# Token sums of the last stage taken from the transposes' PSUM, waits that order GpSimd, and conversions all in the second stage

## Chip, cores and metric

One core of a Trainium2 chip. Times are device microseconds of that core; a run is the time of one whole execution. The kernel before has a median of 644.73 us over 3 runs (643.39 to 645.41).

## What is computed

Three stages follow one another on 1152 tokens of 512 features:

```python
x = window_attention(q, k, v)                 # 2 x 8 heads, 576 positions, window of 64
p = probs / probs.sum(-1)                     # 4 experts
y = sum(p[:, e] * (relu(x @ w1[e]) @ w2[e]) for e in range(4))   # 512 -> 1024 -> 512
h = y @ w_in                                  # 512 -> 2048
out = (h * cos(h)) @ w_out                    # 2048 -> 512
```

The inputs are float32, but `w_in` and `w_out` come as 64-bit floats and are turned into 32-bit ones on the chip.

## The kernel before

**Arithmetic.** Every matmul is done three times: each operand is split into a high part (rounded to the fast 32-bit type) and a low part (the remainder), and high x high, high x low and low x high are added in PSUM. ScalarE writes the high parts and VectorE or GpSimd the low ones.

**Stages.** Attention is a script written out by hand. After it the work is cut into chunks `c` of 512 hidden features: chunks 0 to 7 (NM = 8) are the mixture of experts (two per expert), chunks 8 to 11 the last stage. Tokens are cut into two sets `k`: set 0 has 640 tokens (n = SN[0] = 320 columns in each half, 5 tiles of 128) and set 1 has 512 (n = 256, 4 tiles). A visit (c, k) has two units `u`, and a unit is a first product (`a_unit`) and a second (`b_unit`). The sets alternate: (7,1), (7,0), (8,1), (8,0) are the visits around the turn from the experts to the last stage.

**First product.** `a_unit` multiplies 2 x 2 blocks with seven block products instead of eight (p1 to p7, of 6 matmuls each, at L1049). Product 1 reads the first half of the tokens (`xhi`, `xlo`, features 0 to 255), 2 the same tokens with features 256 to 511, 3 the second half with features 256 to 511, and 5, 6, 7 and 4 read sums of token blocks: `tsum` is formed from `xhi` and `xlo`, and its high and low parts go to `xhi`/`xlo` (second half, features 0 to 255) and `thi`/`tlo`. `t_jobs` makes these sums: for each group of up to 128 columns eight additions or subtractions in a chain (L963, L972), two casts on ScalarE (L985), two remainders (L988). They run on VectorE or GpSimd.

**After the first product** come ReLU in the experts (L1141) and in the last stage `h * cos(h)` (`cos_post`: L1157, L1162, L1168, L1169, L1174, L1177, L1183, three of them on VectorE). `b_unit` then multiplies by the second weights into accumulators (L1236, 6 matmuls per token tile and unit), and `evict` adds these to `acc` on VectorE.

**The turn.** After chunk 7, `turn` transposes each token tile of `acc` into PSUM (`psx`, L1304); ScalarE writes `xhi` (L1312) and VectorE `xlo` (L1317), scaled by 1/2π. Then `t_jobs` makes the sums from `xhi` + `xlo` and all products of (8, k) wait for all of them. For both sets these sums wait for `cos_ready` too, the point from which the last stage's buffers exist; it comes after the conversions.

**Conversions.** Each 64-bit weight unit is loaded, put together from its words on VectorE (L737, L743, L753, L759, L770, with one step on ScalarE, L750, and one sum on GpSimd or VectorE, L765), and stored to DRAM as 32 bits (L776). Twelve of the 16 units run in the experts' stage as 24 parts of 512 columns; the last four (`late_conversions`) run in the last stage as 16 parts of 256. Loads and stores go over SyncE's queue, with the weights.

**Order.** A planner in the kernel's Python makes jobs with an engine, an estimated duration and predecessors, plays them through on a model of the engines and emits each engine's instructions in the order in which the jobs began there. TensorE's list is fixed up to a look-ahead of 8. A job made by `either` may go to VectorE or GpSimd. Jobs marked `port` (GpSimd's, and VectorE's with operands in SBUF alone) never overlap in the plan, but nothing on the chip holds GpSimd to that: it starts as soon as its own inputs are there. GpSimd takes no job in the plan while more than QUIET port jobs of VectorE are ready. `Slots` counts buffers (raws 4, banks 3, accs 4, tsums 2) and `Hold` keeps one of them until its last user is done.

Of the kernel before, what the change touches and what calls it, by code (L numbers as in the profile page):

```python
# [26 lines left out]
def tile_window_attention_moe_cosglu(  # L27
# [13 lines left out]
    P = 128  # L41
# [22 lines left out]
    GC = [G0[g] - S0[SG[g]] for g in range(NG)]  # L64

# [263 lines left out]
    def att_xhi(u):  # L329
        pv, at = o_t[u], (u - 1) * W  # L330
        k = max(i for i in range(2) if S0[i] <= at)
        if at == S0[k]:
            x_tiles(k)
        o = at - S0[k]
        o_t[u] = pv, xhi[k][:, :, o:o + P], xlo[k][:, :, o:o + P]
        nc.scalar.copy(out=xhi[k][:, :, o:o + P], in_=pv)
# [80 lines left out]
    def emit_a(s):  # L417
# [15 lines left out]
        hh = hp.tile([P, 640], F32R, tag="hh", name="hh")[:, :n]  # L433
        hl = hp.tile([P, 640], F32R, tag="hl", name="hl")[:, :n]
        side("h", relu_high, ps, hh)
        side("j", relu_low, s, ps, hh, hl)
# [4 lines left out]
    def relu_low(s, ps, hh, hl):  # L441
# [3 lines left out]
        h_t[s] = (hh, hl)  # L445

    def emit_b(s):
# [6 lines left out]
        for i in range(no):  # L454
            cs = slice(P * i, P * (i + 1))
# [6 lines left out]
            ops = ((hh[:, cs], whi[:, fo, :]), (hh[:, cs], wlo[:, fo, :]), (hl[:, cs], whi[:, fo, :]))  # L462
# [104 lines left out]
    def mm_ns(n):  # L567
        return 13.4 + n / 2.4
# [29 lines left out]
    tsums = Slots(2)  # L598
# [11 lines left out]
    def std_a(s):  # L610
# [18 lines left out]
        def high():  # L629
            box["hh"] = hp.tile([P, 640], F32R, tag="hh", name="hh")[:, :n]  # L630
            relu_high(box["ps"], box["hh"])

        def low():
            hl = hp.tile([P, 640], F32R, tag="hl", name="hl")[:, :n]
            relu_low(s, box["ps"], box["hh"], hl)
# [76 lines left out]
    LATE = 4 * NU // 2  # L712

    def conversion(i, part, parts, name, ready):
        e, kind, u = units[len(units) - NCV + i]
        n = KD * 256 // parts
        box = {}

        def load():
            pool = late_pools[name]  # L720
            t = pool.tile([P, n], U64, tag="raw64", name="raw64", bufs=2)
            src = unit_src(e, kind, u)
            w = src.shape[2]
            if n >= w:
                src = src[:, n // w * part:n // w * (part + 1)]
            else:
                c, f = divmod(n * part, w)
                src = src[:, c:c + 1, f:f + n]
            nc.sync.dma_start(out=t.rearrange("p (a b) -> p a b", b=min(n, w)), in_=src)
# [3 lines left out]
        def words():  # L733
            pool = late_pools[name]
            m = box["m"] = pool.tile([P, n], U32, tag="m64", name="m64", bufs=2)
            box["x"] = pool.tile([P, n], F32, tag="x64", name="x64", bufs=2)
            nc.vector.tensor_scalar(  # L737
# [4 lines left out]
        def sign():  # L742
            nc.vector.scalar_tensor_tensor(  # L743
# [8 lines left out]
        def power():  # L752
            nc.vector.tensor_scalar(  # L753
# [4 lines left out]
        def low():  # L758
            nc.vector.scalar_tensor_tensor(  # L759
# [4 lines left out]
        def total(engine):  # L764
            engine.tensor_tensor(  # L765
# [3 lines left out]
        def guard():  # L769
            nc.vector.scalar_tensor_tensor(  # L770
# [7 lines left out]
        a = job("SP", 500, load, [ready, conv_r[-2]], tail=4500.0)  # L778
# [12 lines left out]
    if wide:  # L791
        for i in range(NCV - LATE):
            for part in range(2):
                conversion(i, part, 2, "w64", swapped)

    def swap_cos():
# [5 lines left out]
            tc.tile_pool(name="tsum", bufs=2, side="right", reuse_waits="tile")  # L802
        )

    def swap_late():
        tctx.close()
        late_pools["late64"] = tctx.enter_context(
            tc.tile_pool(name="late64", bufs=1, side="right", reuse_waits="tile")
        )

    tctx = ExitStack()
    own_sums = []
# [30 lines left out]
    def w1_jobs(x, m):  # L843
# [12 lines left out]
        def sums(i):  # L856
            def fn(engine):
# [8 lines left out]
                engine.tensor_tensor(out=o, in0=a, in1=b, op=op)  # L866
# [21 lines left out]
        def low(i):  # L888
            def fn(engine):
                engine.tensor_tensor(  # L890
# [20 lines left out]
    def w2_jobs(x, m):  # L911
# [20 lines left out]
        def low(i):  # L932
            def fn(engine):
                engine.tensor_tensor(  # L934
# [13 lines left out]
    def t_jobs(k, deps_of, own=False):  # L948
        n, ready = SN[k], []

        def columns(a, w):
            c1, c2 = slice(a, a + w), slice(n + a, n + a + w)
            k1, k2 = slice(0, 2), slice(2, 4)
            hold, box = Hold(tsums if own else raws), {}

            def whole(o, ks, cs):
                def fn(engine):
                    if o == 0:
                        box["t"] = (
                            late_pools["tsum"].tile([P, 4, 2, w], F32, tag="tsum", name="tsum")  # L960
                            if own else rawp.tile([P, 4, 2, w], F32, tag="raw", name="tsum")
                        )
                    engine.tensor_tensor(  # L963
# [5 lines left out]
            def less(o, i, j):  # L969
                def fn(engine):  # L970
                    t = box["t"]
                    engine.tensor_tensor(  # L972
# [21 lines left out]
            for fn in (  # L994
                whole(0, k1, c2), whole(1, k2, c2), less(2, 1, 0), whole(3, k1, c1),
                less(0, 0, 3), less(1, 1, 0), whole(3, k2, c1), less(3, 3, 1),
# [8 lines left out]
            if own:  # L1005
                own_sums.extend(ready)
# [12 lines left out]
    def a_unit(q, c, k, u):  # L1019
# [4 lines left out]
        xr = x_ready.get((c, k), [])  # L1024
        t1, t2 = slice(0, n), slice(n, 2 * n)
# [4 lines left out]
        def rhs(i):  # L1030
# [4 lines left out]
                4: lambda: (thi[k][:, 2], tlo[k][:, 2]),  # L1035
                5: lambda: (xhi[k][:, k1, t2], xlo[k][:, k1, t2]),
                6: lambda: (thi[k][:, 0], tlo[k][:, 0]),
                7: lambda: (thi[k][:, 1], tlo[k][:, 1]),
# [20 lines left out]
        p5 = pe(ns, product(5, "y2", True), [wr[2], *xr], new=[y2])  # L1059
# [16 lines left out]
        p6 = pe(ns, product(6, "z"), [c1, wr[2]], use=zu)  # L1076
# [517 lines left out]
```

## Time and profile before

| | before |
|---|---|
| median of 3 runs | 644.73 us |
| profiled execution, its own time | 645.19 us |
| its span, first to last instruction | 643.4 us |
| VectorE busy | 482.5 us |
| ScalarE busy | 333.0 us |
| GpSimd busy | 224.3 us |
| mean granted TensorE clock | 0.991 of full speed |

The span is what the trace covers; 1.8 us of the profiled execution lie around it. Times in the trace count from the span's start. "PEclk" is the granted clock of TensorE as a share of 2.4 GHz, so 0.50 is 1.2 GHz. "PE" is TensorE's matmul row, "DVE" VectorE, "ACT" ScalarE, "POOL" GpSimd, "SP" SyncE. A figure in square brackets is the time that an engine stood idle just before an instruction, with the engine that released it.

### The profile page before, as it was taken

Reading aid. Unit: us, or ns where it says so; the run is one execution under the profiler, and the core shown is the slowest. Engines: PE = TensorE matmul, PEld = TensorE weight load, DVE = VectorE, ACT = ScalarE, POOL = GpSimd, SP = SyncE. Lnnn points to the kernel's source line nnn. Section 1 sums busy time; section 2 is a strip of 40 time slices with the busy share of each in tenths; the row PEclk is TensorE's granted clock in tenths of the full one; section 3 lists DMA queues with packets and bytes.
Section 4 is the critical chain, followed back from the end, with each engine's and each line's share of the span. In section 5 each row is a group of like instructions: output and inputs, shape, how many; then the busy total and the mean of one; then the engine's idle time right before and its main releaser. Section 6 shows DMA issues by size and latency. Waiting matters only on the chain.

```text
span 643.4 us, 10901 instructions
## 1 busy us (share of the span) xinstructions
PE 625.2 (97%) x4019; PEld 552.8 (86%) x4019; DVE 482.5 (75%) x982; ACT 333.0 (52%) x836; POOL 224.3 (35%) x232
## 2 busy tenths in 40 slices
PE   8999999999999999999999999999699999999997
PEld 7878898889898998888999899988599888989786
DVE  5858535656998888798899753698777798797764
ACT  5957312333353443343443342448598878777563
POOL 6985202211331263253433331355014245134010
PEclk9999999999999999999999999999699999999999
DMA  8943200250055426444445021011204212121112
GB/s 271 309 144 107 76 1 0 99 197 0 1 167 151 141 83 198 146 136 151 141 136 191 35 98 34 13 34 53 66 1 139 92 50 82 51 83 50 49 65 85
DMA packets 39048, 63.12 MB, mean 98 GB/s; under 512 B 3017, under 2 KB 20937, under 8 KB 38994
## 3 DMA queue, kind: packets, MB, share of 16 engines
q1 hardware_dynamic: 38178, 61.63, 30.5%
q10 hardware_dynamic: 816, 0.79, 0.4%
q8 instruction: 31, 0.51, 0.3%
q14 instruction: 23, 0.19, 0.1%
HBM read 51.66 MB, written 10.75 MB: 97 GB/s over the span
## 4 chain that ended last, share of the span: by engine, by line
PE 77%; DVE 11%; ACT 5%; issue 3%; DMA 2%; POOL 1%; POOLq 0%; SPq 0%; DVEq 0%; ACTq 0%
PE pb_acc L1236 30%; PE y L1049 17%; PE seed L1049 13%; PE pb_acc L465 7%; PE ph L624 3%; ACT e L281 1%; DVE tsum L972 1%; PE ph L428 1%; PE ph L429 1%; PE ph L430 1%; DMA raw<-in_moe_w_dram 1%; PE psv L321 1%; DVE acc L476 1%; ACT kk L1169 1%; PE pss L257 1%
## 5 line engine op out<-in xcount | busy, mean ns | idle before, releaser
L1236 PE MATMUL pb_acc<-wlo,hh 128*128 128x512 f32 x360 | 141.7, 394 | 0.3 <-POOL wlo L934 0.3
L1236 PE MATMUL pb_acc<-whi,hh 128*128 128x512 f32 x360 | 141.6, 393 | 0.0
L1236 PE MATMUL pb_acc<-whi,hl 128*128 128x512 f32 x360 | 140.3, 390 | 0.0
L1049 PE MATMUL y<-xhi,w7hi 128*128 128x256 f32 (+1 forms) x320 | 96.2, 301 | 5.2 <-DVE hl L1183 4.2
L765 POOL TENSOR_TENSOR x<-x,m 128x512 f32<-128x512 f32 (+1 forms) x35 | 41.8, 1193 | 163.4 <-DVE x L759 158.5
L1049 PE MATMUL y<-xlo,w7hi 128*128 128x256 f32 (+1 forms) x320 | 95.5, 298 | 0.4 <-DVE xlo L988 0.4
L1049 PE MATMUL y<-xhi,w7lo 128*128 128x256 f32 (+1 forms) x320 | 95.3, 298 | 0.0
L1236 PEld LDWEIGHTS pb_acc<-whi,hl 128*128 128x128 f32 x360 | 67.6, 188 | 15.3
L1049 PE MATMUL seed<-thi,w7hi 128*128 128x320 f32 (+1 forms) x240 | 72.8, 303 | 4.0 <-DVE y L1080 2.8
L1236 PEld LDWEIGHTS pb_acc<-wlo,hh 128*128 128x128 f32 x360 | 67.8, 188 | 9.8 <-POOL wlo L934 0.9
L1236 PEld LDWEIGHTS pb_acc<-whi,hh 128*128 128x128 f32 x360 | 67.7, 188 | 9.6
L1049 PE MATMUL seed<-thi,w7lo 128*128 128x320 f32 (+1 forms) x240 | 71.0, 296 | 0.0
L1049 PE MATMUL seed<-tlo,w7hi 128*128 128x320 f32 (+1 forms) x240 | 70.9, 295 | 0.0
L1049 PEld LDWEIGHTS y<-xhi,w7hi 128*128 128x128 f32 x320 | 61.1, 191 | 8.2 <-DVE hl L1183 5.2
L1049 PEld LDWEIGHTS y<-xlo,w7hi 128*128 128x128 f32 x320 | 61.2, 191 | 2.4 <-DVE xlo L988 0.7
L1049 PEld LDWEIGHTS y<-xhi,w7lo 128*128 128x128 f32 x320 | 61.0, 191 | 0.0
L476 DVE SCALAR_TENSOR_TENSOR acc<-pb_acc,gate_p,acc 128x512 f32<-128x512 f32 x63 | 46.3, 743 | 12.9 <-PE pb_acc L1236 12.1
L1049 PEld LDWEIGHTS seed<-thi,w7hi 128*128 128x128 f32 x240 | 45.3, 189 | 12.1 <-DVE y L1080 5.0
L934 POOL TENSOR_TENSOR wlo<-raw,whi 128x512 fp32r<-128x512 f32 x22 | 30.4, 1396 | 64.4 <-ACT whi L929 64.4
L1049 PEld LDWEIGHTS seed<-tlo,w7hi 128*128 128x128 f32 x240 | 45.4, 189 | 3.6
L890 POOL TENSOR_TENSOR w7lo<-sums,w7hi 128x512 fp32r<-128x512 f32 x23 | 32.4, 1410 | 43.0 <-ACT w7hi L885 26.3
L1049 PEld LDWEIGHTS seed<-thi,w7lo 128*128 128x128 f32 x240 | 45.4, 189 | 0.0
(133 smaller groups left out, 1358.9 us busy)
## 6 DMA issues: line engine op xcount, KB each, us to landing
raw<-in_moe_w_dram SPq DMA_DIRECT2D x32, 512.0 KB, 5.1
raw<-w SPq DMA_DIRECT2D x16, 512.0 KB, 3.3
raw<-in_moe_w_in_dram SPq DMA_DIRECT2D x12, 512.0 KB, 4.3
w<-x SPq DMA_DIRECT2D x24, 256.0 KB, 4.4
raw<-in_moe_w_out_dram SPq DMA_DIRECT2D x12, 512.0 KB, 4.1
vr<-in_v_dram SPq DMA_DIRECT2D x16, 256.0 KB, 4.1
out_dram<-acc SPq DMA_DIRECT2D x18, 128.0 KB, 1.7
qraw<-in_q_dram SPq DMA_DIRECT2D x16, 128.0 KB, 3.8
```

Source lines behind the costliest of these rows:

```text
L257: nc.tensor.matmul(out=out[h][W * c:W * (c + 1), p], lhsT=qts[c][rows, p, :], rhs=kts[c][rows, p, :], start=True, stop=True,)
L281: nc.scalar.activation(out=e[:, p], in_=s[:, p], func=AF.Exp, bias=nm[:, p:p + 1], scale=1.0, accum_out=sm[:, p:p + 1],)
L321: nc.tensor.matmul(out=pv[W * h:W * (h + 1), p, W * c:W * (c + 1)], lhsT=vts[c][:, P * p + W * h:P * p + W * (h + 1)], rhs=pts[h][:, p, W ...
L428: nc.tensor.matmul(out=ps, lhsT=whi[:, d, cs], rhs=xh[:, d, :], start=d == 0, stop=False)
L465: nc.tensor.matmul(out=ps, lhsT=a, rhs=b, start=first and m == 0, stop=last and m == 2)
L476: nc.vector.scalar_tensor_tensor(out=a, in0=ps, scalar=p, in1=a, op0=ALU.mult, op1=ALU.add)
L624: nc.tensor.matmul(out=ps, lhsT=a[:, d, cs], rhs=b[:, d, :], start=d == 0 and m == 0, stop=d == KD - 1 and m == 2,)
L765: engine.tensor_tensor(out=box["x"], in0=box["x"], in1=box["m"].bitcast(F32), op=ALU.add)
L890: engine.tensor_tensor(out=operand(w_lo[x], i), in0=part(i), in1=operand(w_hi[x], i).bitcast(F32), op=ALU.subtract,)
L934: engine.tensor_tensor(out=w_lo[x][:, i], in0=box["t"][:, i], in1=w_hi[x][:, i].bitcast(F32), op=ALU.subtract,)
L1049: nc.tensor.matmul(out=ps, lhsT=a[:, WI[i], d, :], rhs=b[:, d, :], start=start and d == 0 and m == 0, stop=d == 1 and m == 2, skip_group_c ...
L1236: nc.tensor.matmul(out=ps, lhsT=a[:, cs], rhs=b[:, fo, :], start=first and fo == 0 and m == 0, stop=last and fo == 1 and m == 2,)
```

## The change

- **Token sums.** `turn` now writes to `xhi` and `xlo` only what products 1, 2 and 3 read (the first half, and features 256 to 511 of the second half). A new `token_sums` forms the sums of one column group of w columns (w = 64 for set 0, 5 groups; 128 for set 1, 2 groups) as soon as the two transposed tiles that it needs are there: one ScalarE copy from PSUM, two VectorE subtractions that read PSUM, one ScalarE cast and one remainder for product 5 (`s0`), two subtractions, one cast and one remainder for products 4, 6 and 7 (`s1`). The transposes' PSUM banks (`accs`) are held until then. Set 1's sums use the weights' raw buffers and no longer wait for `cos_ready`; set 0's have 4 buffers instead of 2.
- **Products of (8, k)** wait each for what they read: 1 and 2 for `h4`, `l4`; 5 also for `s0`; 6 also for `s1`; 3 also for `h2`, `l2`.
- **Token tiles of the last expert chunk** are done in rising order.
- **Conversions.** All 16 units run as 32 parts of 512 in the experts' stage; `late_conversions` goes.
- **Order.** Each `port` instruction on GpSimd gets a wait for the last VectorE `port` instruction before it in the plan. QUIET goes from 2 to 1. The planner's price of a matmul becomes a table.
- **No other work.** The operand order in `t_jobs` and the layout of the hidden tiles are rewritten; functions return their instruction so that the wait can be added.

```diff
+    def tokens(t, k, i):
+        return t[..., P * i:P * (i + 1)]
...
     def mm_ns(n):
-        return 13.4 + n / 2.4
+        return {256: 118.3, 320: 147.0, 384: 173.5, 512: 230.5}[n]
...
-    tsums = Slots(2)
+    tsums = Slots(4)
...
-        for i in range(NCV - LATE):
+        for i in range(NCV):
             for part in range(2):
-                conversion(i, part, 2, "w64", swapped)
+                conversion(i, part)
...
-            tc.tile_pool(name="tsum", bufs=2, side="right", reuse_waits="tile")
+            tc.tile_pool(name="tsum", bufs=4, side="right", reuse_waits="tile")
...
-    def late_conversions():
-        ready = job(None, 0.0, swap_late, [cos_ready, *own_sums])
-        conv_last[:], conv_r[:] = [ready, ready], [ready, ready]
-        if wide:
-            for i in range(NCV - LATE, NCV):
-                for part in range(4):
-                    conversion(i, part, 4, "late64", ready)
...
+        if c == NM:
+            parts = [(what, j) for (kk, i, what), j in x_parts.items() if kk == k]
+            def of(*names):
+                return [j for what, j in parts if what in names]
+            xr = of("h4", "l4")
...
-        p5 = pe(ns, product(5, "y2", True), [wr[2], *xr], new=[y2])
+        p5 = pe(ns, product(5, "y2", True), [wr[2], *xr, *of("s0")], new=[y2])
...
-        p6 = pe(ns, product(6, "z"), [c1, wr[2]], use=zu)
+        p6 = pe(ns, product(6, "z"), [c1, wr[2], *of("s1")], use=zu)
...
-        p3 = pe(ns, product(3, "y2"), [u4, wr[3]], use=[y2])
+        p3 = pe(ns, product(3, "y2"), [u4, wr[3], *of("h2", "l2")], use=[y2])
...
-        for rank, i in enumerate([*range(no - 1, n // P - 1, -1), *range(n // P)]):
+        turn_here = c == NM - 1 and u == NU - 1
+        row = [*range(no - 1, full - 1, -1), *range(full)]
+        for i in sorted(row) if turn_here else row:
...
+    def token_sums(k, i, c, w, s):
+        t1, hold1, box1, of1 = s["first"]
+        t2, hold2, box2, of2 = s["second"]
+        hold, old = Hold(raws if w == P else tsums), products[NM - 1, k]
...
+        f = job("ACT", act_ns(4 * w), whole, [t1, None if w == P else cos_ready], new=[hold], use=[hold1])
+        a = job("DVE", dve_ns(2 * w), from_psum(0, k1, 1), [f, t2], use=[hold2, hold])
+        h = job("ACT", act_ns(2 * w), sum_high(0), [a, *old], use=[hold])
+        x_parts[k, c, "s0"] = either(2 * w, sum_low(0), [h], use=[hold])
+        a = job("DVE", dve_ns(2 * w), from_psum(3, k2, 0), [a, t2], use=[hold2, hold])
+        b3 = either(2 * w, less(1, 3, 1), [a], use=[hold])
+        b4 = either(2 * w, less(2, 2, 3), [a], use=[hold])
+        h = job("ACT", act_ns(6 * w), sum_high(1), [b3, b4, *old], use=[hold])
+        x_parts[k, c, "s1"] = either(6 * w, sum_low(1), [h], use=[hold])
...
-        if c == NM and (c, k) not in x_ready:
...
-            x_ready[c, k] = t_jobs(k, deps_of, True) + [
-                j for (kk, i, what), j in x_parts.items() if kk == k and what == "l"
-            ]
...
-    QUIET = 2
+    QUIET = 1
...
+    ahead = None
     for j in sorted(jobs, key=lambda j: (began[j], rank[j])):
-        if j.size:
-            j.fn(nc.vector if j.eng == "DVE" else nc.gpsimd)
-        else:
-            j.fn()
+        made = j.fn(nc.vector if j.eng == "DVE" else nc.gpsimd) if j.size else j.fn()
+        if j.port and j.eng == "POOL" and ahead:
+            tc.add_manual_dep(
+                made.ins, ahead.ins.name,
+                mybir.DependencyInfo(mybir.DependencyClass.Sync, mybir.DependencyReason.DATA),
+                reason="one engine at a time",
+            )
+        elif j.port:
+            ahead = made
```

## Rows read from the trace of the kernel before

**Rows 1.** Page part 1: busy time, share of the span and instructions of TensorE.

```profile
PE 625.2 (97%) x4019; PEld 552.8 (86%) x4019; DVE 482.5 (75%) x982; ACT 333.0 (52%) x836; POOL 224.3 (35%) x232
```

**Rows 2.** TensorE's timeline at the turn: start us, us, what [idle before <-releaser].

```profile
451.56 0.39 PE L1236 MATMUL pb_acc<-whi,hl 128*128 128x512 f32 x1
456.18 0.63 PE L1049 MATMUL y<-xhi,w7hi 128*128 128x320 f32 x1 [4.23 <-DVE hl L1183]
...
464.97 0.31 PE L1049 MATMUL y<-xhi,w7lo 128*128 128x320 f32 x1
```

**Rows 3.** Chain that ended last: start us, us, what; one product and one token tile.

```profile
470.68 1.39 PE pb_acc L1236 x6
...
477.44 0.88 PE y L1049 x6
```

**Rows 4.** Windows: length, busy time per engine (PE PEld DVE ACT POOL), PEclk, DMA.

```profile
452.00:454.00 2.00, 0.00 (x0) 0.00 (x0) 1.97 (x7) 0.86 (x3) 0.00 (x0) 1.00 0.00 0
454.00:456.00 2.00, 0.00 (x0) 0.00 (x0) 2.00 (x5) 1.03 (x3) 0.00 (x0) 0.66 0.00 0
...
464.00:466.00 2.00, 2.00 (x10) 1.87 (x10) 0.62 (x2) 0.53 (x1) 0.00 (x0) 0.78 0.20 80
```

**Rows 5.** VectorE's timeline at the turn, columns as in rows 2.

```profile
446.86 2.85 DVE L972 TENSOR_TENSOR tsum<-tsum 128x128 f32<-128x128 f32 x2
...
451.38 0.55 DVE L988 TENSOR_TENSOR tlo<-tsum,thi 128x384 fp32r<-128x384 f32 x1
...
459.58 0.42 DVE L988 TENSOR_TENSOR xlo<-tsum,xhi 128x256 fp32r<-128x256 f32 x1
```

**Rows 6.** GpSimd's timeline at the turn, columns as in rows 2.

```profile
446.83 2.60 POOL L934 TENSOR_TENSOR wlo<-raw,whi 128x512 fp32r<-128x512 f32 x2
```

**Rows 7.** Windows as in rows 4, longer stretches.

```profile
180.00:420.00 240.00, 239.48 (x1413) 215.32 (x1412) 191.19 (x346) 94.05 (x212) 84.59 (x73) 1.00 0.40 122
420.00:440.00 20.00, 19.54 (x116) 17.29 (x116) 17.87 (x32) 12.62 (x28) 8.28 (x9) 1.00 0.16 54
440.00:460.00 20.00, 13.80 (x80) 11.43 (x78) 19.85 (x45) 13.81 (x34) 7.55 (x10) 0.87 0.00 1
```

**Rows 8.** VectorE by form: busy us, mean ns, idle before.

```profile
L770 DVE SCALAR_TENSOR_TENSOR x<-raw,x 128x512 f32<-128x512 f32 x24 | 22.9, 954 | 6.9 <-POOL x L765 6.9
L743 DVE SCALAR_TENSOR_TENSOR m<-raw,m 128x512 uint32<-128x512 uint32 x24 | 18.6, 774 | 0.2
...
L759 DVE SCALAR_TENSOR_TENSOR x<-raw,x 128x512 f32<-128x512 uint32 x24 | 17.0, 707 | 0.3
...
L753 DVE TENSOR_SCALAR x<-m 128x512 uint32<-128x512 uint32 x24 | 11.0, 460 | 0.2
L737 DVE TENSOR_SCALAR m<-raw 128x512 uint32<-128x512 uint32 x24 | 10.5, 436 | 0.0
...
L1080 DVE TENSOR_TENSOR y<-seed,p 128x256 f32<-128x256 f32 x20 | 8.5, 424 | 7.5 <-PE seed L1049 3.3 <-ACT w7hi L885 2.1 <-issue 2.0
...
L988 DVE TENSOR_TENSOR xlo<-tsum,xhi 128x256 fp32r<-128x256 f32 x8 | 3.3, 414 | 0.0
```

**Rows 9.** GpSimd by form, columns as in rows 8.

```profile
L934 POOL TENSOR_TENSOR wlo<-raw,whi 128x512 fp32r<-128x512 f32 x22 | 30.4, 1396 | 64.4 <-ACT whi L929 64.4
```

**Rows 10.** GpSimd's and VectorE's busy time of L765 alone, in a window.

```profile
180.00:420.00 240.00, 3.80 (x3) 25.40 (x19) 1.00 0.40 122
```

**Rows 11.** VectorE's timeline: the first and the last of the 24 L770 of 512.

```profile
176.10 1.43 DVE L770 SCALAR_TENSOR_TENSOR x<-raw,x 128x512 f32<-128x512 f32 x1
...
361.40 1.21 DVE L770 SCALAR_TENSOR_TENSOR x<-raw,x 128x512 f32<-128x512 f32 x1 [0.40 <-POOL x L765]
```

**Rows 12.** ScalarE's timeline: the first cosine step of the last stage.

```profile
432.37 0.47 ACT L1157 ACTIVATE kk<-y,bias_m 128x256 f32<-128x256 f32 x1 [1.06 <-PE y L1049]
```

**Rows 13.** Waits of TensorE from 560 us on: total us, times, longest.

```profile
PE seed L1049 <- ACT seed L1063: 0.7, 1, 0.7
...
PE pb_acc L1236 <- POOL wlo L934: 0.3, 1, 0.3
```

More of the change, by code (lines that the diff above doesn't have):

```diff
@@ L953, in columns @@
             k1, k2 = slice(0, 2), slice(2, 4)
-            hold, box = Hold(tsums if own else raws), {}
+            hold, box = Hold(raws), {}
             def whole(o, ks, cs):
@@ L958, in fn @@
                     if o == 0:
[L959 to L963, printed above, removed]
+                        box["t"] = rawp.tile([P, 4, 2, w], F32, tag="raw", name="tsum")
+                    return engine.tensor_tensor(
                         out=box["t"][:, o], in0=xhi[k][:, ks, cs].bitcast(F32),
@@ L1306, in transposes, with columns, high, fn @@
                 )
-        def high():
-            if (k, "x") not in begun:
-                begun.add((k, "x"))
-                x_tiles(k)
+        def columns(cs, second):
+            a = w * cs[0] + (n if second else 0)
+            return slice(a, a + w * len(cs)), slice(a - P * i, a - P * i + w * len(cs))
+        def high(cs, second):
+            def fn():
+                if (k, "x") not in begun:
+                    begun.add((k, "x"))
+                    x_tiles(k)
+                ks = k2 if second else slice(0, KD)
+                to, of = columns(cs, second)
+                nc.scalar.activation(
+                    out=xhi[k][:, ks, to], in_=box["pv"][:, ks, of], func=AF.Copy,
+                    scale=1.0 / TWO_PI,
+                )
+            return fn
@@ new lines, in low, with fn, keep @@
+        def low(cs, second):
+            def fn():
+                ks = k2 if second else slice(0, KD)
+                to, of = columns(cs, second)
+                nc.vector.scalar_tensor_tensor(
+                    out=xlo[k][:, ks, to], in0=box["pv"][:, ks, of], scalar=1.0 / TWO_PI,
+                    in1=xhi[k][:, ks, to].bitcast(F32), op0=ALU.mult, op1=ALU.subtract,
+                )
+            return fn
+        def keep(what, j):
+            x_parts[k, i, what] = j
+            return j
@@ new lines, in turn @@
+        t = keep("t", pe(4 * 112.0, transposes, [evicted[k, i]], new=[hold]))
+        turn_after[b] = t
+        old = products[NM - 1, k]
+        for cs, second in ((c1, False), (c2, True)):
+            if not cs:
+                continue
+            ks = 2 if second else KD
+            m = ks * w * len(cs)
+            h = keep(f"h{ks}", job("ACT", act_ns(m), high(cs, second), [t, *old], use=[hold]))
+            keep(f"l{ks}", job("DVE", dve_ns(m), low(cs, second), [h], use=[hold]))
+            for c in cs:
+                s = sums_of.setdefault((k, c), {})
+                if second:
+                    s["second"] = t, hold, box, columns([c], True)[1]
+                else:
+                    s["first"] = t, hold, box, columns([c], False)[1]
+                if len(s) == 2:
+                    token_sums(k, i, c, w, s)
```

188 lines of the change are left out of this document (104 added, 84 removed).

## Prediction, made before the change was run

> **What bounds the kernel now.** I read the engines' shares first: TensorE is busy 625.2 of 643.4 us, 97% [rows 1], so a gain has to come out of its idle time or its clock. Its timeline shows where: around 451.6 to 465 us, the turn from the experts to the last stage. The last matmul of the old work starts at 451.56 us, the next at 456.18 after 4.23 us of idling, and the 24th from the turn on starts at 464.97 [rows 2]. These 24 are four products of set 0 (1, 5, 6, 2). A product of 6 matmuls takes 0.88 us at full clock, a token tile of 6 takes 1.39 [rows 3], a matmul thus 0.147 and 0.23 us. From 451.56 + 0.23 = 451.79 to 464.97 + 0.147 = 465.12 are 13.33 us for work of 4 x 0.88 = 3.52: **9.8 us are lost at this one place**. Part is idling, the rest the clock: it stands at full speed in 452 to 454 us, at 0.66 in 454 to 456 and 0.78 in 464 to 466 [rows 4]. Between only two levels, 2.4 and 1.2 GHz, that means a fall after about 2.8 us of idling (at 454.6) and a return at 464.9.
>
> What is late is VectorE. It is busy 19.85 of 20 us in 440 to 460 [rows 7], and runs the token sums of set 0 from 446.86 to 460.00 us [rows 5], in between seven cosine steps of set 1. At their head two short sums take 2.85 us together [rows 5]; GpSimd's two remainders run from 446.83 to 449.43 [rows 6]. A remainder of 384 columns takes 0.55 us [rows 5], one of 256 takes 0.41 [rows 8], so 128 columns cost about 0.28 (an estimate, from these two) and the pair should take 0.56: VectorE stood blocked for some 2.3 us.
>
> **Token sums and the products' waits.** The work hardly shrinks. A group of 64 columns has five VectorE operations of 128 columns and one of 384: 5 x 0.28 + 0.55 = 1.95 us, five groups 9.8 us if VectorE does all. Before, the stretch of 13.1 us, less seven cosine steps of about 0.42 [rows 8] (2.9 us) and the block of 2.3, held 7.9 us of sums, and GpSimd had done others. `xlo` becomes 640 of 2560 columns shorter, some 0.65 us. So VectorE would be through with everything at about 460.0 - 2.3 - 0.65 + 1.9 = 459 us. ScalarE gets five copies of 256 columns, but is busy only 13.8 of 20 us there [rows 7].
>
> The gain is in the order. Product 1 needs no sum now, product 5 only each group's first third, and groups begin when their two tiles are transposed instead of after all. From 451.8 us TensorE has products 1, 5 and 2 (3 x 0.88) and the left-over tile of (8,1)'s second product (1.39): 4.0 us that wait for no `s1`, to 455.8. Cosine steps of 2.9 us in VectorE's stretch can go behind the sums, which then end at 459 - 2.9 = 456. Remaining loss: at best 0; at worst, with the cosine steps left between, 459 + 0.5 (the last product's release) - 455.8 = 3.7 us. I take **1.5 us**, nearer the better end since the planner puts first what TensorE's list wants first. The idling stays under the 2.8 us after which the clock fell, so the clock stays up. Term: 1.5 - 9.8 = **-8.3 us**.
>
> What is late next is the cosine work of (8,1), which feeds TensorE two slots later. The PSUM banks held longer are the second thing: four `accs` serve five transposes and the four accumulators of (8,1).
>
> Reading PSUM costs VectorE little here: 424 ns for 256 columns with one operand in PSUM against 414 with both in SBUF [rows 8], so ten such operations add 0.1 us. The Trainium skill (Perfetto Trace Analysis, section Optimizing Scalar/DVE Operations) gives a fixed cost of about 125 ns on PSUM against 60 on SBUF; ten operations would add 0.65 us by it and the remaining loss would be about 2.1 us instead of 1.5. The rows decide.
>
> **Conversions.** Removed from the last stage: 16 parts with 16 loads and 16 stores on SyncE's queue. TensorE waits there after 560 us for 0.7 us on ScalarE and 0.3 on GpSimd [rows 13]; bounds 0 to -1, I take -0.5. Added to the experts' stage: 8 parts of 512. One costs VectorE 954 + 774 + 707 + 460 + 436 ns = 3.33 us [rows 8], together 26.6 us. The cover: between 180 and 420 us VectorE is free for 240 - 191.2 = 48.8 us [rows 7]. Without it every microsecond would push the cosine buffers back. SyncE's queue now holds these parts' loads and stores, each waiting for VectorE, ahead of weight loads of chunks 7 and 8. The first and the last of 24 parts end 185.3 us apart [rows 11], 8.1 us each; eight more at that pace end at about 427 us, against the first cosine step at 432.37 [rows 12]. Tight, but VectorE is emptier at the end. Bounds 0 and +7 (below); I take +0.5.
>
> **Waits on GpSimd, QUIET and the rest.** Behind a waiting GpSimd instruction stand its next weight remainders and sums; ScalarE's casts of sums and TensorE's products wait for these. TensorE's only long-run wait for GpSimd is 0.3 us [rows 13], so the slack is there but its size is not shown. Bounds: a gain up to the 2.3 us block (counted above), a loss up to one VectorE operation of 0.7 us at each spot without slack. I take 0. Matmul prices, tile layout and operand names change no instruction: 0.
>
> **Sum.** -8.3 - 0.5 + 0.5 = -8.3 us on the profiled 645.19 gives 636.9; that execution lay 0.46 us above the median, so **636.4 us**.
>
> **Rivals.**
> 1. *The block only moves.* GpSimd waits for VectorE, never the reverse. Its remainder, 1.3 us, can still be running when VectorE's next sum comes, as at 446.83 [rows 5, 6]; the 2.3 us come back at the turn: 636.4 + 2.3 = 638.7. The Trainium skill (SBUF — State Buffer, section Who interferes with whom) says so too: who issues first holds the shared port for a whole instruction. The trace agrees with its 2.85 us. Against: fewer jobs go to GpSimd. 10%.
> 2. *The banks or VectorE leave a gap of about 3 us.* The accumulators of (8,1) need banks that the sums hold, and VectorE is full. Then the clock falls again; of the 9.8 us, 4.2 idled before the first product, so the clock and the short gaps made up to 5.6. With 1.3 fewer idle there and a few short ones gone, some 7 us stay lost: 642.0. 12%.
> 3. *The sums end no earlier,* because VectorE is simply full (17.87 of 20 us in 420 to 440, 19.85 in 440 to 460 [rows 7]) and TensorE's list runs into the cosine steps instead: 644.7. That the waits do not hold GpSimd back is the same case. 10%.
> 4. *Slower: VectorE runs out in the experts' stage.* With QUIET at 1 and conversions always ready, GpSimd's weight work goes to VectorE: 84.59 - 25.40 = 59.2 us there [rows 7, 10], at 774 ns instead of 1396 [rows 8, 9] 32.8 us. With 26.6 for the conversions that is 59.4 against 48.8 free, 10.6 short, and no room until 460 us. The turn's relief on VectorE (2.3 + 0.65 + some 0.5) pays 3.4; 7.2 us remain: 651.9. It decides from a shortage of 3.4 + 1.9 = 5.3 us, when 27.5 of the 32.8 us move. For: the 24 parts before end at 362 us [rows 11], so much of the room lies late, after weights are due. Against: TensorE's list goes first in the plan, and less GpSimd work stretches VectorE less. 16%.
>
> **How the numbers follow.** Forecast 52%, rivals 10, 12, 10 and 16%. 0.3% (1.9 us) is about what a measurement tells from no change: faster is below 642.8, slower above 646.7. The forecast, rival 1 and three quarters of rival 2 are faster (0.71, I say 0.70), the rest of 2 and most of 3 the same (0.13), rival 4 and a tail of 3 slower (0.17). The forecast's own range is 633 to 639. The range given starts at 633.0 (all 9.8 us, the 1.0 after 560 and some short gaps of TensorE gone) and reaches to 646.5, over rivals 1 to 3, which leaves rival 4 and little else outside.
>
> **What would show it.** Right: TensorE's gap at the turn under 2 us and no stretch at 0.50; the products of (8,0) released by the sums one after another; the last L770 before about 432 us and none after; little L765 or `tsum` work on GpSimd at the turn. Wrong: TensorE waiting for L1157's chain near 430 us, a gap of 3 us or more with the clock down, VectorE at 10 tenths between 340 and 420 us, or new waits of TensorE for GpSimd's L890 and L934.

## The result, and the profile after

The changed kernel has a median of 639.12 us (638.07 to 639.75, 4 runs) against 644.62 us before (one run more than above): a ratio of 0.9915, with a 95% interval from 0.9893 to 0.9936. It is 5.5 us faster; 8.3 were forecast. The profiled execution took 639.75 us with a span of 637.8.

Most of the reading below uses one sum: the **lost time** of TensorE. It is worked out from TensorE's timeline: the distance from each matmul's start to the next one's, less what that distance is when work is there and the clock is full (0.2285 us for 512 columns, 0.1463 for 320, 0.1187 for 256, and some 0.36 for the four transposes of a token tile). It holds idling and slow clock alike. The stretches are bounded by times of the trace, and each row is one execution. The last two columns are that execution's time and the median of the kernel's runs.

| us lost in | 100-140 | 140-400 | 400-480 (turn) | 480-560 | 560-640 | this execution, us | median, us |
|---|---|---|---|---|---|---|---|
| before | 0.5 | 3.4 | 12.8 | 0.4 | 3.8 | 645.2 | 644.6 |
| **after** | **5.3** | **2.9** | **7.2** | **0.3** | **0.2** | **639.8** | **639.1** |
| waits alone | 0.5 | 1.5 | 10.6 | 0.3 | 3.1 | 640.1 | 639.9 |
| after, no waits | 6.1 | 3.9 | 6.8 | 0.3 | 0.2 | 641.8 | 642.0 |
| after, QUIET 2 | 0.4 | 5.4 | 6.3 | 0.3 | 0.3 | 635.7 | 637.2 |
| token sums alone | 0.5 | 1.9 | 7.8 | 1.4 | 2.7 | 639.4 | 637.3 |
| after, late conversions | 5.0 | 1.7 | 4.9 | 1.6 | 0.7 | 637.6 | 637.8 |
| after, old prices | 5.4 | 3.1 | 6.2 | 0.3 | 0.5 | 641.0 | 640.2 |
| all but token sums | 5.0 | 4.8 | 9.0 | 0.4 | 0.2 | 645.4 | 643.0 |
| **token sums and waits** | **0.5** | **1.3** | **4.7** | **1.3** | **1.5** | **633.9** | **633.6** |
| the same, QUIET 1 | 5.5 | 1.6 | 5.0 | 1.7 | 2.0 | 639.2 | 639.2 |
| the same, early conversions | 0.5 | 3.0 | 7.7 | 0.3 | 0.6 | 638.0 | 635.2 |
| the same, new prices | 0.5 | 1.9 | 5.7 | 1.0 | 1.9 | 634.7 | 634.6 |
| the same, QUIET 3 | 0.5 | 3.8 | 2.6 | 0.5 | 7.1 | 638.3 | 637.6 |

So the change won 5.6 us at the turn, 3.6 after 560 us and 0.5 in the experts' stage, and gave 4.8 away in a place where little had been lost before.

Two things limit what rows of the table can be compared for. The stage before 100 us, which the change leaves alone, is not in it: the first `ph` matmul of 512 columns starts at 96.4 us in one execution (experiment 3) and at 99.4 in another (experiment 7). And the clock at the turn fell in five of the executions (before, after, waits alone, token sums alone, early conversions) and not in the other nine. So a difference of 2 us between two rows need not be the edit's; the medians decide.

**The shares.** From the page of the changed kernel, the busy times of part 1, and the granted clock of part 2 in 40 slices:

```profile
PE 622.8 (98%) x4019; PEld 553.2 (87%) x4019; DVE 470.6 (74%) x990; ACT 335.2 (53%) x840; POOL 156.9 (25%) x169
...
PEclk9999999899999999999999999999899999999999
```

TensorE's share went from 97% [rows 1] to 98%. GpSimd lost 67 us of busy time, VectorE 12; the waits alone take as much off VectorE with its instructions unchanged (experiment 1). The clock now falls twice, in slices 8 and 29.

**The turn.** TensorE's timeline after, then its windows with the columns of rows 4:

```profile
452.68 0.28 PE L1037 MATMUL seed<-thi,w7lo 128*128 128x256 f32 x1
455.26 0.52 PE L1231 MATMUL pb_acc<-whi,hh 128*128 128x512 f32 x1 [2.30 <-DVE xlo L1328]
```

```profile
452.00:454.00 2.00, 0.96 (x8) 0.72 (x6) 2.00 (x10) 1.94 (x6) 0.00 (x0) 1.00 0.00 0
454.00:456.00 2.00, 0.74 (x2) 0.63 (x3) 2.00 (x8) 1.97 (x7) 0.00 (x0) 0.88 0.00 0
456.00:458.00 2.00, 2.00 (x7) 1.60 (x6) 2.00 (x6) 1.96 (x5) 0.00 (x0) 0.50 0.04 8
458.00:460.00 2.00, 2.00 (x10) 1.86 (x10) 1.99 (x8) 0.41 (x1) 1.06 (x1) 0.76 0.00 0
```

The gap of 4.23 us [rows 2] is one of 2.30, and the half-rate stretch is about 3.4 us long (0.24, 1 and 0.48 of three windows of 2 us: twice what each PEclk lacks to 1, since half rate counts a half) where it had been 10.2. What ends the gap is new. Before, it was product 1 of (8,0), and not a sum was what it waited for: the releaser is `hl` of L1183 [rows 2], the last cosine step on one of (8,1)'s `y`, and sums ran on until 460.00 us [rows 5], 3.8 us after that product had begun. VectorE before:

```profile
455.71 0.41 DVE L1183 SCALAR_TENSOR_TENSOR hl<-y,hh 128x256 fp32r<-128x256 f32 x1
```

That step is the last to read this `y` from PSUM; it ends at 456.12, and the product, which begins a new `y`, has its bank. The wait of all products for all sums was thus one of the plan, which sets the order, and not of the chip.

Now the gap ends with a token tile of (8,1), `pb_acc`, that waits for `xlo` on VectorE. It does not read that `xlo`. It needs the PSUM bank that the transposed tile still holds, and this is VectorE's timeline there:

```profile
454.30 0.48 DVE L1387 TENSOR_TENSOR tsum<-tsum 128x128 f32<-128x128 f32 x2
454.70 0.41 DVE L1328 SCALAR_TENSOR_TENSOR xlo<-psx,xhi 128x256 fp32r<-128x256 f32 x1
...
455.36 0.42 DVE L1172 SCALAR_TENSOR_TENSOR hl<-y,hh 128x256 fp32r<-128x256 f32 x1
```

By these times, moving that tile back would have won little: the first products of (8,0) need one of three other banks, all held by the last unit of (8,1), and the first of them comes free with the `hl` at 455.36 us, which ends at 455.78.

VectorE is as full as before (`DVE` is 2.00 of 2 us in three of the four windows above, 19.4 of 20 in 440 to 460).

**The new loss near 115 us.** TensorE's timeline, then VectorE's, of the changed kernel; the last row is VectorE before, in the same place:

```profile
114.08 0.39 PE L469 MATMUL pb_acc<-whi,hl 128*128 128x512 f32 x1
117.39 0.63 PE L469 MATMUL pb_acc<-whi,hh 128*128 128x512 f32 x1 [2.92 <-DVE acc L480]
```

```profile
101.11 1.42 DVE L944 TENSOR_TENSOR tsum<-xhi,xlo 128x256 f32<-128x256 f32 x4
...
110.25 1.40 DVE L480 SCALAR_TENSOR_TENSOR acc<-pb_acc,gate_p,acc 128x512 f32<-128x512 f32 x2
...
116.59 0.74 DVE L480 SCALAR_TENSOR_TENSOR acc<-pb_acc,gate_p,acc 128x512 f32<-128x512 f32 x1
```

```profile
107.80 2.07 DVE L476 SCALAR_TENSOR_TENSOR acc<-pb_acc,gate_p,acc 128x512 f32<-128x512 f32 x3 [0.57 <-PE pb_acc L465]
```

This is the start of the second scheme of the experts' stage, where set 0's first token sums are made. Before, three accumulators were emptied in a row at 107.8 us. After, VectorE does the sums, empties two at 110.25, does more sums and weight work, and empties the third at 116.59. TensorE's next group needs four banks, gets three and stands for 2.92 us, and the first matmul behind the gap takes 0.63 us instead of 0.39: the clock fell.

**Conversions and the port.** VectorE by form after, then GpSimd by form, with the columns of rows 8:

```profile
L770 DVE SCALAR_TENSOR_TENSOR x<-raw,x 128x512 f32<-128x512 f32 x32 | 21.3, 682 | 2.6 <-POOL x L765 2.6
```

```profile
L918 POOL TENSOR_TENSOR wlo<-raw,whi 128x512 fp32r<-128x512 f32 x20 | 26.4, 1328 | 78.5 <-ACT whi L913 43.8 <-DVE xlo L1403 19.9 <-DVE x L770 7.2
```

All 32 parts are there, and L770 takes 682 ns where it took 954 [rows 8]; GpSimd's remainder takes 1328 instead of 1396 [rows 9]. Its waits now name VectorE. The window from 180 to 420 us, columns as in rows 7:

```profile
180.00:420.00 240.00, 239.27 (x1419) 215.84 (x1420) 210.64 (x419) 100.59 (x225) 52.81 (x47) 1.00 0.47 147
```

VectorE is busy for 19.4 us more than before [rows 7], GpSimd for 31.8 less. The last L770 is at 402.7 us, the first cosine step at 435.4.

### The profile page after: what moved, and what is told of

Same layout as the page of the kernel before. It is cut to its first block, busy times and chain, and to the rows that moved or that the text cites. A ratio compares the mean times of both kernels' runs of the same rounds, so it can differ in the third digit from the quotient of the medians.

```text
span 637.8 us, 10837 instructions
## 1 busy us (share of the span) xinstructions
PE 622.8 (98%) x4019; PEld 553.2 (87%) x4019; DVE 470.6 (74%) x990; ACT 335.2 (53%) x840; POOL 156.9 (25%) x169
## 4 chain that ended last, share of the span: by engine, by line
PE 85%; DVE 7%; ACT 3%; DMA 2%; issue 1%; POOL 1%; DVEq 0%; SPq 0%; POOLq 0%
PE pb_acc L1231 37%; PE y L1037 19%; PE seed L1037 14%; PE pb_acc L469 7%; PE ph L628 2%; ACT e L284 1%; PE ph L431 1%; PE ph L433 1%; PE ph L432 1%; DMA raw<-in_moe_w_dram 1%; PE psv L324 1%; DVE acc L480 1%; PE pss L260 1%; PE pst L309 1%; DVE tsum L944 1%
## 5 line engine op out<-in xcount | busy, mean ns | idle before, releaser
L1037 PE MATMUL seed<-thi,w7hi 128*128 128x320 f32 (+1 forms) x240 | 71.4, 298 | 2.0 <-DVE y L1068 1.0
L874 POOL TENSOR_TENSOR w7lo<-raw,w7hi 128x256 fp32r<-128x256 f32 (+1 forms) x21 | 17.9, 856 | 139.0 <-DVE sums L850 50.3
L444 ACT ACTIVATE hh<-y 128x320 fp32r<-128x320 f32 (+1 forms) x48 | 19.5, 407 | 50.2 <-PE y L1037 50.1
L918 POOL TENSOR_TENSOR wlo<-raw,whi 128x512 fp32r<-128x512 f32 x20 | 26.4, 1328 | 78.5 <-ACT whi L913 43.8
```

The costliest lines, as they stand in the source:

```text
L444: nc.scalar.activation(out=hh, in_=ps, func=AF.Relu)
L874: return engine.tensor_tensor(out=operand(w_lo[x], i), in0=part(i), in1=operand(w_hi[x], i).bitcast(F32), op=ALU.subtract,)
L918: return engine.tensor_tensor(out=w_lo[x][:, i], in0=box["t"][:, i], in1=w_hi[x][:, i].bitcast(F32), op=ALU.subtract,)
L1037: nc.tensor.matmul(out=ps, lhsT=a[:, WI[i], d, :], rhs=b[:, d, :], start=start and d == 0 and m == 0, stop=d == 1 and m == 2, skip_group_c ...
```

## Experiments

Theory A is the prediction's, with one thing added after the result: the gain is in the order of the sums at the turn and in the conversions that leave the last stage, the waits are worth little (both the prediction's), and QUIET at 1 made the loss near 115 us (added). Each verdict has the ratio to the kernel before with its 95% interval.

**1. The waits alone.** The kernel before, with the loop that adds them; no engine's order changes.

```diff
+        if j.port and j.eng == "POOL" and ahead:
+            tc.add_manual_dep(made.ins, ahead.ins.name, ...)
+        elif j.port:
+            ahead = made
```

> The kernel before with the GpSimd waits alone; every engine's order stays as it was. Theory A (the waits only tidy the port, the gain is in the order of the sums and in the conversions that leave the last stage): VectorE's blocked operations shrink (the mean of L770 at 512 columns from 954 ns to below 800, the 2.85 us pair at the turn to about 0.6), the turn gains at most the 2.3 us block, 642 to 645 us. Rival B (the waits are what made the change faster): 639 to 641 us.

Measured: 639.9 us, 0.9931 (0.9909 to 0.9954). Theory A missed this: the waits alone are worth some 4 us. VectorE's timeline at the turn and its L770:

```profile
444.07 1.11 DVE L972 TENSOR_TENSOR tsum<-tsum 128x128 f32<-128x128 f32 x2
```

```profile
L770 DVE SCALAR_TENSOR_TENSOR x<-raw,x 128x512 f32<-128x512 f32 x24 | 18.9, 787 | 6.9 <-POOL x L765 6.9
```

The pair that took 2.85 us [rows 5] takes 1.11. GpSimd's two remainders, at 446.83 before [rows 6], start at 453.84 and 456.33 now. The turn's lost time falls by 2.2 us, about the block that the prediction had measured. But 1.9 us came from the experts' stage and 0.7 from the last, of which the prediction had nothing. The order of every engine is unchanged, and over the whole run VectorE is busy for 470.4 us instead of 482.5 [rows 1] with the same 982 instructions, GpSimd for 213.3 instead of 224.3 with the same 232. So the two held each other up less, and TensorE behind them.

**2. The changed kernel without the waits.** Again no order changes.

```diff
-        if j.port and j.eng == "POOL" and ahead:
+        if False and j.port and j.eng == "POOL" and ahead:
```

> The changed kernel without the GpSimd waits; every engine's order stays as it is. Theory A: within 1.5 us of the changed kernel (638 to 641 us), and the new gap of TensorE of 2.9 us near 115 us stays, since it comes from the order. Rival B: 642 us or more at the turn; and if the waits caused the gap near 115 us, it goes and the time is 635 to 636 us.

Measured: 641.95 us, 0.9963 (0.9943 to 0.9983), 2.8 us more than the changed kernel and nearly twice the allowance of 1.5. The wait near 115 us stays, in the list of TensorE's waits between 100 and 125 us:

```profile
PE pb_acc L469 <- DVE acc L480: 3.7, 1, 3.7
```

The turn's sum hardly differs (6.8 against 7.2 us lost), but the clock fell there with the waits only. A block is there without them, in VectorE's timeline, then GpSimd's:

```profile
449.96 1.58 DVE L1387 TENSOR_TENSOR tsum<-tsum 128x128 f32<-128x128 f32 x2
```

```profile
449.97 1.42 POOL L918 TENSOR_TENSOR wlo<-raw,whi 128x512 fp32r<-128x512 f32 x1 [9.52 <-ACT whi L913]
```

The same pair takes 0.48 us with the waits (at 447.04). Before 400 us the waits save 0.8 and 1.0 us in the table. L770's mean is 798 ns without them.

**3. QUIET back at 2.**

```diff
-    QUIET = 1
+    QUIET = 2
```

> The changed kernel with QUIET back at 2. Theory A (QUIET at 1 puts the first token sums and weight sums on VectorE, so that an accumulator is emptied late near 115 us): GpSimd takes some of set 0's first sums again, the gap near 115 us goes, 634 to 637 us. Rival C (the gap comes from the table of matmul prices or from the waits): the gap stays, 639 to 641 us. Should QUIET at 1 be what opens room at the turn, the gap at the turn grows past 3 us and the time is 640 us or more.

Measured: 637.21 us, 0.9877 (0.9844 to 0.991). The gap near 115 us is gone (0.4 us lost instead of 5.3), so Theory A holds there. 2.5 us more are lost between 140 and 400, and the time is just above the expected band.

**4. The token sums alone.** The changed kernel, less:

```diff
-    QUIET = 1
+    QUIET = 2
...
-        if j.port and j.eng == "POOL" and ahead:
+        if False and j.port and j.eng == "POOL" and ahead:
...
-        return {256: 118.3, 320: 147.0, 384: 173.5, 512: 230.5}[n]
+        return 13.4 + n / 2.4
...
+        if c == NX - 1 and (k, u) == (visits[2 * (c - SPL)][1], 0):
+            late_conversions()
```

> Of the change only the token sums from PSUM, the products' own waits and the rising order of tiles; late conversions, no waits, QUIET 2 and the old matmul prices as before. Theory A: what is lost between 400 and 480 us falls from 12.8 to about 7 us, TensorE's waits after 560 us (some 3.5 us lost) stay, no gap near 115 us: 638 to 640 us. Rival B: the turn gains under 2 us without the waits, 643 to 645 us.

Measured: 637.32 us, 0.989 (0.9855 to 0.9925): a little under the band, and not slower than the whole change. The turn loses 7.8 us instead of 12.8. TensorE's timeline, VectorE's and GpSimd's there:

```profile
454.14 0.64 PE L1060 MATMUL y<-xhi,w7hi 128*128 128x320 f32 x1 [2.58 <-DVE hl L1195]
```

```profile
447.18 1.35 DVE L1410 TENSOR_TENSOR tsum<-tsum 128x128 f32<-128x128 f32 x1
```

```profile
447.08 1.31 POOL L941 TENSOR_TENSOR wlo<-raw,whi 128x512 fp32r<-128x512 f32 x1 [0.66 <-ACT whi L936]
```

A single operation of 128 columns takes 1.35 us and ends at 448.53, just behind GpSimd's at 448.39: without the waits the block is there again. The product of (8,0) waits for `hl` here too, the bank of a cosine step.

**5. Late conversions back** in the changed kernel.

```diff
+        if c == NX - 1 and (k, u) == (visits[2 * (c - SPL)][1], 0):
+            late_conversions()
```

> The changed kernel with the last four units' conversions back in the last stage (16 parts of 256). Theory A: what TensorE loses after 560 us goes from 0.3 us to 2 to 3.5 us, as in the kernel before and in the run with the waits alone; the gap near 115 us and the turn stay: 641 to 643 us. Rival: the conversions are hidden anyway and the last stage is quiet through the waits or the freer VectorE: 638.5 to 640 us.

Measured: 637.76 us, 0.9899 (0.9882 to 0.9916). A miss: 1.4 us less than the changed kernel, though the intervals overlap. From 480 us on 2.3 us are lost instead of 0.5, as expected in kind, but the turn loses 4.9 instead of 7.2 and the experts' stage 1.7 instead of 2.9. Moving the conversions moved the loss.

**6. Old matmul prices** in the changed kernel.

```diff
-        return {256: 118.3, 320: 147.0, 384: 173.5, 512: 230.5}[n]
+        return 13.4 + n / 2.4
```

> The changed kernel with the planner's old formula for a matmul. Theory A (the gap near 115 us comes from QUIET at 1): it stays, 638 to 641 us. Rival C (the new prices make the planner empty an accumulator late): it goes, 634 to 636 us.

Measured: 640.23 us, 0.9934 (0.9915 to 0.9954). The gap near 115 us stays (3.07 us), so it does not come from the prices.

**7. All but the token sums**: the kernel before with waits, QUIET 1, the prices and all conversions early.

```diff
-    QUIET = 2
+    QUIET = 1
...
-        for i in range(NCV - LATE):
+        for i in range(NCV):
...
-        return 13.4 + n / 2.4
+        return {256: 118.3, 320: 147.0, 384: 173.5, 512: 230.5}[n]
...
+            tc.add_manual_dep(made.ins, ahead.ins.name, ...)
```

> The kernel before with everything of the change except the token sums: waits, QUIET 1, the table of prices and all conversions in the experts' stage. Theory A: the loss between 400 and 480 us is 9 to 12 us instead of 7, the gap near 115 us and the quiet last stage are those of the changed kernel: 642 to 645 us. Rival (the waits alone mend the turn, the token sums add nothing): 638.5 to 640 us.

Measured: 643.04 us, 0.9977 (0.9959 to 0.9994), inside the band. Inside the whole change the token sums are worth 3.9 us; the rest together is worth 1.6, less than its waits alone.

**8. Token sums and waits**: experiment 4 with the waits back.

```diff
-        if False and j.port and j.eng == "POOL" and ahead:
+        if j.port and j.eng == "POOL" and ahead:
```

> The token sums of the run with these alone, with the GpSimd waits added; every engine's order as in that run (late conversions, QUIET 2, old prices). If the waits help also where the block at the turn is gone (the 2 us in the experts' stage that the run with the waits alone won): 634.5 to 636.5 us. If the two remove the same block: 637 to 638 us. If the waits delay GpSimd at the turn, 638.5 us or more.

Measured: 633.6 us (632.75 to 635.0), 0.9835 (0.9816 to 0.9855), below all three expected cases. This beats both kernels; its interval lies clear of the changed kernel's. TensorE's gaps at the turn, from its timeline:

```profile
438.80 0.39 PE L1060 MATMUL y<-xhi,w7hi 128*128 128x256 f32 x1 [0.72 <-DVE hl L1195]
...
440.76 0.39 PE L1060 MATMUL seed<-thi,w7hi 128*128 128x256 f32 x1 [0.54 <-ACT seed L1074]
...
451.04 0.42 PE L1060 MATMUL y<-xhi,w7hi 128*128 128x320 f32 x1 [1.52 <-DVE hl L1195]
```

No gap over 1.52 us, the first matmul behind it takes 0.42 us: the clock stayed up. Token sums and waits add up. At the turn the loss goes from 12.8 to 7.8 by the sums and on to 4.7 with the waits, and after 480 us from 4.1 to 2.8 with the waits. How much of the step from 7.8 to 4.7 is the waits' is not shown: the execution of experiment 4 lay 2.0 us above its median, and its clock fell at the turn. In two of that kernel's four runs the mean granted clock is 1.000, so it cannot have fallen in them for 3.4 us.

The last four take this kernel and add one part each.

**9. QUIET 1.**

```diff
-    QUIET = 2
+    QUIET = 1
```

> The run with token sums and waits (633.6 us), with QUIET 1 instead of 2 and nothing else. Theory A: TensorE waits some 3 us for an accumulator near 115 us with the clock down behind it, 4 to 5 us lost there, nothing of it elsewhere: 637 to 639 us. Rival: without the 32 early parts and with the old prices VectorE has the room, the gap does not come and the time stays at 633 to 635 us.

Measured: 639.22 us, 0.9917 (0.9903 to 0.9932), just above the band: 5.6 us more, of which 5.0 are lost near 115 us. VectorE's timeline and TensorE's there:

```profile
107.74 0.75 DVE L480 SCALAR_TENSOR_TENSOR acc<-pb_acc,gate_p,acc 128x512 f32<-128x512 f32 x1
116.06 1.40 DVE L480 SCALAR_TENSOR_TENSOR acc<-pb_acc,gate_p,acc 128x512 f32<-128x512 f32 x2
```

```profile
116.86 0.49 PE L469 MATMUL pb_acc<-whi,hh 128*128 128x512 f32 x1 [3.07 <-DVE acc L480]
```

One accumulator is emptied early and two late: the same wait as in the changed kernel, from QUIET alone.

**10. All conversions early.**

```diff
-            late_conversions()
...
-        for i in range(NCV - LATE):
+        for i in range(NCV):
```

> The run with token sums and waits (633.6 us), with all conversions in the experts' stage and nothing else. The last stage's loss (some 2.5 us from 500 us on) goes. If the experts' stage hides the eight parts more: 631 to 632.5 us. If they come back as waits of TensorE for VectorE between 160 and 430 us and at the turn (as the run with QUIET 2 suggests, which lost 3.5 us between 280 and 400 us): 634.5 to 637 us.

Measured: 635.24 us, 0.9865 (0.9842 to 0.9887), in the second band; it overlaps the interval of experiment 8. From 480 us on 0.9 us are lost instead of 2.8, in the experts' stage 3.0 instead of 1.3 and at the turn 7.7 instead of 4.7:

```profile
454.62 0.63 PE L1037 MATMUL y<-xhi,w7hi 128*128 128x320 f32 x1 [2.68 <-DVE hl L1172]
```

This execution lay 2.8 us above its median, in part through the clock, which fell behind the gap, and the stage before 100 us, 2.0 us longer than in experiment 8's; the shortest of the five runs took 634.19 us with a mean granted clock of 1.000. How much of the 3.0 us at the turn the early conversions cost is thus not settled.

**11. The table of matmul prices.**

```diff
-        return 13.4 + n / 2.4
+        return {256: 118.3, 320: 147.0, 384: 173.5, 512: 230.5}[n]
```

> The run with token sums and waits (633.6 us), with the table of matmul prices and nothing else. The prices only reorder: within 1.5 us of 633.6 us, no gap near 115 us. Rival: part of what the changed kernel gives away comes from them, 636 us or more.

Measured: 634.57 us, 0.9849 (0.9832 to 0.9865), within the allowance, no gap near 115 us.

**12. QUIET 3.**

```diff
-    QUIET = 2
+    QUIET = 3
```

> The run with token sums and waits (633.6 us), with QUIET 3: GpSimd may take work while three port jobs of VectorE are ready. If GpSimd's help is what keeps VectorE off TensorE's path, 631.5 to 633.5 us; if the port is what counts, VectorE is held up longer behind GpSimd's 1.3 us operations and the time is 635 us or more.

Measured: 637.63 us, 0.989 (0.9874 to 0.9907). The time is as in the second case but not for its reason: the turn loses only 2.6 us. 7.1 are lost after 560 us, in the last chunk, where TensorE waits for weight parts (its waits between 595 and 615 us) and then runs at half rate, PEclk 0.50 from 606 to 612 us:

```profile
PE pb_acc L1254 <- ACT whi L936: 1.9, 1, 1.9
PE pb_acc L1254 <- POOL wlo L941: 0.7, 1, 0.7
```

## Why the prediction was right, and where not

**Right: the place and the direction.** The loss at the turn was where the gain came from; 639.1 lies in the range of 633.0 to 646.5, just above the forecast's own 633 to 639. The token sums alone take 5.0 us off the turn's lost time (experiment 4), and without them the rest of the change is nearly worthless (7).

**Term "-8.3 us" for the turn: mis-sized.** It measured -5.6 in the changed kernel (12.8 to 7.2 lost). The step that failed was the cover: "TensorE has products 1, 5 and 2 and the left-over tile of (8,1)'s second product: 4.0 us that wait for no `s1`". None of it was free to run: it waits for PSUM banks, the tile for one held by a transposed tile until 455.11 us, the products for one held by the cosine steps of (8,1) until 455.78. So "Cosine steps of 2.9 us in VectorE's stretch can go behind the sums" was wrong as well, since these steps free the products' banks. The prediction took the gap of 4.23 us for a wait for sums; rows 2 name `hl`, a cosine step, and the same wait ends the turn's longest gap in experiments 1, 3 to 6 and 8 to 11. The runs show that the sums from PSUM win time at the turn (4, 7); that they do it by letting VectorE come to that step earlier is argued from these rows, not shown. The banks held by transposes are the second thing that the prediction named as late next, and the mechanism of rival 2, which had 12%. With QUIET 2, the old prices and late conversions (8) the term is -8.1: sums and waits together can do what was forecast, but not beside the rest of this change.

**"The idling stays under the 2.8 us after which the clock fell, so the clock stays up": wrong.** The gap was 2.3 us and the clock fell in the window of its end. The last section returns to it. Three of the prediction's own signs of being right thus failed at the turn: a gap under 2 us, no stretch at 0.50, products released by the sums. Those on the conversions and on GpSimd came true: the last L770 is at 402.7 us, and GpSimd has no L765 or `tsum` work at the turn.

**"Waits on GpSimd ... I take 0": wrong.** They are worth some 4 us alone (1), 2.8 within the change (2) and 3.7 on top of the token sums (8 against 4, whose intervals just touch). The bound, "a gain up to the 2.3 us block", was read off the turn alone. VectorE was held up all through the experts' stage, as L770's mean of 954 ns against 682 shows [rows 8]: before, single ones took from 0.67 to 1.78 us. The prediction used that mean as the price of the work and did not ask what was in it. Rival 1 (the block only moves) fell: in experiment 1 a trace of it remains, 1.11 us for the pair instead of 0.56, and single L770 there still take up to 1.48 us.

**QUIET, in the same 0: wrong by more.** It costs 5.6 us (9). Rival 4 had QUIET make the kernel slower, through VectorE running out of time between 180 and 420 us. VectorE did not run out: it is busy 210.6 of 240 us there. The loss is at 115 us, before the stretch that was looked at, and comes from the order: VectorE does the sums that GpSimd had done, and accumulators are emptied behind them. All six kernels with QUIET 1 lose 5.0 to 6.1 us there, all eight with 2 or 3 lose 0.4 or 0.5. Why the planner puts the emptying that late was not tried.

**Conversions: "-0.5" and "+0.5".** The last stage won 3.6 us after 560, more than the bound of 1. That bound took two waits of rows 13; a third, 0.5 us for VectorE's `y` (L1080), stands between them, and the short gaps around the three are not in the list. The waits on GpSimd share in this (3.8 to 3.1 with them alone). The experts' stage and the turn seem to give it back: within the change (5 against the changed kernel) and on the best kernel (10 against 8) the time is 1.4 and 1.6 us longer with all conversions early, with overlapping intervals both times. The sum of about 0 was right in size; a small loss is likelier than a gain. Its price of 3.33 us for a part holds the blocked L770 and leaves out L765, which VectorE now does for 19 parts (0.72 us each) and did for 3. The conversions were done at 402.7 us, not 427. Being blocked had not set the pace: without the waits they are done at 405.3 (experiment 2). The planner put 32 parts closer than 24, 7.2 us apart instead of 8.1; why was not tried.

**Net.** From the kernel with token sums and waits (633.6), QUIET 1 adds 5.6, early conversions 1.6 and the prices 1.0; together they add 5.5. They are not independent, since each reorders everything behind it. The forecast came out near the truth partly because a gain that it had missed (the waits) and a loss that it had missed (QUIET) offset each other.

## What to carry to other kernels

A mean duration in a profile can hold waiting: compare the shortest and the mean of one form before using it as a price, because the difference is waiting, some of which a change of order may win. Where one engine is fed by a planner, hold the order fixed (add or remove a wait alone) before judging a wait; then add each knob singly, since here the best kernel had two of the change's five parts. A buffer that is held longer shows up as a wait for an engine that looks unrelated, so look at what the released instruction writes to as well as what it reads. One trace is one execution: before a difference between two traces is explained, compare each with the median of its kernel, and a stretch that the edit does not touch.

## Unexpected from the hardware

Which VectorE operations GpSimd holds up is visible in an overlap of the changed kernel at the turn. VectorE's timeline, then GpSimd's:

```profile
447.70 0.68 DVE L1378 SCALAR_TENSOR_TENSOR tsum<-psx,tsum 128x128 f32<-128x128 f32 x3
448.36 0.43 DVE L1163 TENSOR_TENSOR seed<-seed,kk 128x256 f32<-128x256 f32 x1
448.70 0.42 DVE L1068 TENSOR_TENSOR y<-seed,p 128x256 f32<-128x256 f32 x1
449.03 0.61 DVE L1403 TENSOR_TENSOR tlo<-tsum,thi 128x384 fp32r<-128x384 f32 x1
```

```profile
447.92 1.30 POOL L918 TENSOR_TENSOR wlo<-raw,whi 128x512 fp32r<-128x512 f32 x1 [10.23 <-DVE xlo L1403]
```

Beside GpSimd's operation the five with one operand in PSUM (L1378 three times, L1163, L1068) keep their usual length; L1403, with both in SBUF, takes 0.61 us against 0.55 [rows 5] and ends after it. That difference is small; the clear cases are the 2.85 us of [rows 5], the 1.58 us of experiment 2 and the 1.35 us of experiment 4, all with both operands in SBUF. The Trainium skill (SBUF — State Buffer, section Who interferes with whom) says that a VectorE instruction with at most one SBUF input, outside the modes that use both of its ports, does not contend with GpSimd; these rows agree. Sums from PSUM thus also move two of six operations off the shared port.

The clock did not follow the length of the gap alone. In the changed kernel a gap of 2.30 us was followed by 1.2 GHz (the windows above). In experiment 2, with every engine in the same order, the same tile waited 2.25 us and the clock stayed at 1.00. In experiment 3 a longer gap was not followed by it either; TensorE's row and the windows:

```profile
454.21 0.41 PE L1037 MATMUL y<-xhi,w7hi 128*128 128x320 f32 x1 [3.03 <-DVE hl L1172]
```

```profile
450.00:452.00 2.00, 1.18 (x6) 0.62 (x4) 2.00 (x6) 1.97 (x6) 0.00 (x0) 1.00 0.00 0
452.00:454.00 2.00, 0.00 (x0) 0.00 (x0) 2.00 (x8) 2.00 (x6) 0.12 (x1) 1.00 0.00 0
454.00:456.00 2.00, 1.79 (x10) 1.66 (x11) 1.87 (x6) 1.50 (x5) 2.00 (x2) 1.00 0.03 8
456.00:458.00 2.00, 2.00 (x14) 1.87 (x13) 1.95 (x4) 1.80 (x5) 0.42 (x1) 1.00 0.00 0
```

TensorE idled 3.03 us and stayed at 2.4 GHz throughout. That was the fastest of this kernel's four runs; two of the others have a mean granted clock of 0.997 instead of 1.000, about what one stretch of 3.4 us at half rate takes off. So the same instructions can meet the fall in one execution and not in the next. What decides it is open; what a fall costs can be read, some 1.7 us for each 3.4 us at half rate.
